# Wider dense products, paired weight-gradient products and VectorE copies in a two-layer attention decode backward pass

## The chip, the cores and the metric

The kernel runs on one core of a Trainium2 chip. The metric is the device time in microseconds (us) of one execution.

## The reference

Two attention blocks and two feed-forward blocks share their weights (A and B), one token goes through, and the outputs are the result and all gradients. Cut to what matters:

```python
Hq, Hkv, Sk, Dh, D, F = 32, 4, 65536, 128, 1024, 3584      # bf16
def A(x, k_cache, v_cache, wq, wo):                         # one query token
    q = (x @ wq) ...; p = softmax(q @ k.T * Dh**-0.5); return (p @ v) @ wo
def B(x, w1, b1, w2, b2):
    r = relu(x @ w1 + b1); return (r * r) @ w2 + b2
x = x + A(ln(x), ...); x = x + B(ln(x), ...)
x = x + A(ln(x), ...); x = x + B(ln(x), ...)
outputs = x, and vjp(grad_out) for x, k_cache, v_cache, wq, wo, w1, b1, w2, b2
```

The caches are 67 MB each. Both are read in each of four passes, and their gradients (again 134 MB) are written in the last.

## The kernel before

It makes four passes over the caches: forward of layer one, forward of layer three, one backward pass that gives layer three's query gradient, and a last pass that gives layer one's and writes the cache gradients. Between passes lie *dense stages* (one, two and three below) with layer norm, wq, wo, w1 and w2. A weight is loaded in slabs (1 MB or 896 KB pieces). In the views PE is TensorE, the matrix engine, ACT is ScalarE, DVE is VectorE, POOL is GpSimd, and SPq is the queue that issues the loads. Matrix results go to PSUM tiles (`ps_` in the views), and a copy out of one is an eviction. A weight is used in one of two ways. `g_mv` holds a 128x128 block of the weight still and streams the vector, one column wide ("block products"). `Rows` is for products with the transposed weight: it transposes eight blocks on PE, copies them to SBUF and multiplies ("row products"), or does the piece on VectorE, as a balancer decides.

```python
def g_mv(slab_it, nk, nbk, xcol, ps, finish, ...):
    for kc, slab in slab_it:
        for nb in range(nbk):
            nc.tensor.matmul(ps[:, nb:nb + 1], lhsT=cols(slab, nb), rhs=xcol(kc), start=first, stop=last, ...)
        add_load(pe=nbk * 0.064)
# Rows.front: transpose to PSUM, evac (copy) to wt; Rows.back:
for i in range(w):
    nc.tensor.matmul(job["y"][:, kc, q:q + 1], lhsT=wt[:, i, :], rhs=job["vb"][:, k0 + i:k0 + i + 1], ...)
# last pass: outer products of two rows, 512 columns, evicted by ScalarE or VectorE
def rank2(out, ra, rb):
    pg = ps_gg()                                  # four such PSUM tiles, shared with the cache gradients
    nc.tensor.matmul(pg[:, 0:n], lhsT=ra, rhs=rb, start=True, stop=True)
    evac(out, pg[:, 0:n], kind="f32")
# background work of the last pass runs up to six steps ahead of an even spread
while self.normal and self.done < self.total * i / self.steps + 6: ...
```

All 1 MB tiles (cache blocks, slabs, staged outputs) share 12 slots. A slot whose tile was stored is passed over for `STORE_STEPS = 5` steps, and seven cache blocks are kept from one pass to the next.

Of the kernel before, what the change touches and what calls it, by code (L numbers as in the profile page):

```python
# [16 lines left out]
P = 128  # L17
# [3 lines left out]
def kernel(  # L21
# [117 lines left out]
    def evac(out, in_, kind="bf"):  # L139
        n = 1  # L140
        for d in in_.shape[1:]:
            n *= d
        ca = 0.17 + n * 0.00083
        cd = 0.13 + n * (0.00054 if kind == "bf" else 0.00105)
        if load["act"] + ca <= load["dve"] + cd:
            load["act"] += ca
            nc.scalar.copy(out=out, in_=in_)  # L147
        else:
            load["dve"] += cd
            nc.vector.tensor_copy(out=out, in_=in_)  # L150
# [235 lines left out]
    def g_mv(slab_it, nk, nbk, xcol, ps, finish, side=None, pre=None, cols=None):  # L386
        first = True
        for kc, slab in slab_it:
            for nb in range(nbk):
                last = (kc == nk - 1) and (nb == nbk - 1)  # L390
                nc.tensor.matmul(ps[:, nb:nb + 1], lhsT=(cols or d_cols)(slab, nb), rhs=xcol(kc),
                                 start=first, stop=last, skip_group_check=True)
                first = False
            add_load(pe=nbk * 0.064)
            if side is not None:
                side(kc, slab)
            yield
        if pre is not None:
            pre()
        finish(ps)  # L400
        yield
# [57 lines left out]
    class Rows:  # L459
# [23 lines left out]
        def begin(self, job):  # L483
            npc = len(job["pieces"])
            job["vb"] = to_cols_bf(job["vcol"](), job["nj"])
            job["y"] = ps_acc([P, job["nk"], npc]) if PS["pass4"] else ps_bg([P, job["nk"], npc])
            if job["mix"]:
                nc.vector.memset(job["y"][:, :, :], 0.0)
                job["y2"] = tmp.tile([P, job["nk"], npc], F32, name="rows_y2", tag="rows_y2")
                nc.gpsimd.memset(job["y2"][:, :, :], 0.0)  # L490
                if job["vbc"] is None:
                    if npc > 1:
                        job["slot"] = Slot("s_vbc", True)
                        job["vbc"] = bcast_vec(job["vcol"](), job["nj"], job["slot"].t, f=job["cols"] is f_cols)
                    else:
                        job["vbc"] = bcast_vec(job["vcol"](), job["nj"])
                reset_load()

        def front(self, job, kc, slab):
            L = load  # L500
            for q, (k0, w) in enumerate(job["pieces"]):
                pe = w * 0.09
                if job["vbc"] is not None:
                    n = w * P
                    stt = max(L["dve"] + 0.1 + n * 0.00105, L["act"], L["pe"])
                    tra = max(L["dve"], L["act"] + 0.17 + n * 0.00083, L["pe"] + pe)
                    if stt <= tra:
                        if "y" not in job:
                            self.begin(job)
                        junk = mvs.tile([P, 1024], BF, name="mv_junk", tag="mv_t", bufs=2)  # L510
                        nc.vector.scalar_tensor_tensor(out=junk[:, 0:n], in0=slab[:, k0 * P:k0 * P + n], scalar=1.0,
                                                       in1=job["vbc"][:, k0 * P:k0 * P + n], op0=ALU.mult, op1=ALU.mult,
                                                       accum_out=job["y2"][:, kc, q:q + 1])
                        add_load(dve=0.1 + n * 0.00105)
                        self.did(job)
                        continue
                pt = self.ps_wt()
                for i in range(w):
                    nc.tensor.transpose(pt[:, i, :], job["cols"](slab, k0 + i), ident_b[:, :])  # L519
                if self.views:  # L520
                    wt = self.views.popleft()
                else:
                    wt = self.pool.tile([P, 8, P], BF, name="wt", tag="wt", bufs=self.bufs)
                evac(wt[:, 0:w, :], pt[:, 0:w, :])
                add_load(pe=pe)
                self.queue.append((job, kc, q, wt))
                if len(self.queue) >= self.bufs:
                    yield
# [8 lines left out]
        def back(self):  # L537
            job, kc, q, wt = self.queue.popleft()
            k0, w = job["pieces"][q]
            if "y" not in job:  # L540
                self.begin(job)
            for i in range(w):
                nc.tensor.matmul(job["y"][:, kc, q:q + 1], lhsT=wt[:, i, :], rhs=job["vb"][:, k0 + i:k0 + i + 1],
                                 start=(i == 0), stop=(i == w - 1), skip_group_check=True)
            self.did(job)

        def did(self, job):
            nk, npc = job["nk"], len(job["pieces"])
            job["done"] += 1
            if job["done"] == nk * npc:  # L550
                y = job["y"][:, :, :]
                if job["mix"]:
                    ym = tmp.tile([P, nk, npc], F32, name="rows_ym", tag="rows_ym")
                    nc.vector.tensor_tensor(out=ym[:, :, :], in0=y, in1=job["y2"][:, :, :], op=ALU.add)
                    y = ym[:, :, :]
                    if job["slot"] is not None:
                        job["slot"].free()
# [34 lines left out]
    class Background:  # L592
# [8 lines left out]
        def step(self, i):  # L601
# [10 lines left out]
            while self.normal and self.done < self.total * i / self.steps + 6:  # L612
# [76 lines left out]
    def g_q(L, g, ps=None, it=None):  # L689
        def fin(p):  # L690
            nc.vector.tensor_copy(out=L["qT"][:, gsl(g)], in_=p[:, :])
            nc.vector.tensor_copy(out=L["qpad"][:, g, :, :], in_=L["qT"][:, gsl(g)].unsqueeze(1).to_broadcast([P, 8, R]))
        yield from g_mv(it or wq_slabs(g)[0], DC, 8, lambda kc: L["nb"][:, kc:kc + 1],
                        ps_bg([P, 8]) if ps is None else ps, fin)


    def g_wo(L, xacc, g, ps=None, it=None):
        def fin(p):
            nc.vector.tensor_tensor(out=xacc[:], in0=xacc[:], in1=p[:, :], op=ALU.add)
        yield from g_mv(it or wo_slabs(g)[0], R, 8, lambda kc: L["oTb"][:, g * R + kc:g * R + kc + 1],  # L700
                        ps_bg([P, 8]) if ps is None else ps, fin)
# [398 lines left out]
    def rows2(cols, j0, jn, rows, f=False):  # L1100
        cc = tmp.tile([P, 4, 2], BF, name="r2_cc")
        for l in range(2):
            nc.vector.tensor_copy(out=cc[:, 0:jn, l], in_=cols[l][:, j0:j0 + jn])
        pg = ps_gg()
        for jj in range(jn):
            nc.tensor.matmul(pg[0:2, jj * P:(jj + 1) * P], lhsT=cc[:, jj, :], rhs=ident_b[:, :], start=True, stop=True)
        if f:
            evac(rows.rearrange("r (p j) -> r p j", j=4), pg[0:2, 0:jn * P].rearrange("r (j p) -> r p j", j=4), kind="f32")
        else:
            evac(rows, pg[0:2, 0:jn * P], kind="f32")  # L1110

    def rank2(out, ra, rb):
        pg = ps_gg()
        n = out.shape[-1]
        nc.tensor.matmul(pg[:, 0:n], lhsT=ra, rhs=rb, start=True, stop=True)  # L1115
        evac(out, pg[:, 0:n], kind="f32")

    def g_outer(pool, out_dram, nA, nB, a_cols, b_cols, c0=0, a_f=False):

        rb = pool.tile([2, 8 * P], BF, name="rowb", tag="rowb")  # L1120
        for k in range(0, nB, 4):
            rows2(b_cols, k, 4, rb[0:2, k * P:(k + 4) * P])
            yield
        for a0 in range(0, nA, 4):
            ra = pool.tile([2, 4 * P], BF, name="rowa", tag="rowa", bufs=2)
            rows2(a_cols, a0, 4, ra[0:2, :])
# [3 lines left out]
            for j in range(4):  # L1130
                for n0 in range(0, 1024, 512):
                    rank2(og[:, j, n0:n0 + 512], d_cols(ra, j) if a_f else f_cols(ra, j), rb[:, n0:n0 + 512])
# [6 lines left out]
    def g_outer_wide(pool, out_dram, nA, nB, a_cols, b_cols):  # L1139
# [3 lines left out]
        for k in range(0, nB, 4):  # L1143
            rows2(b_cols, k, 4, rb[0:2, k * P:(k + 4) * P], f=True)
            yield
        for a in range(nA):
            if a % 4 == 0:
                ra = pool.tile([2, 4 * P], BF, name="rowa", tag="rowa", bufs=2)
                rows2(a_cols, a, 4, ra[0:2, :])
                yield  # L1150
            sl = Slot("og", True)
            for n0 in range(0, nB * P, 512):
                rank2(sl.t[:, n0:n0 + 512], ra[:, (a % 4) * P:(a % 4 + 1) * P], rb[0:2, n0:n0 + 512])
                if n0 % 1024 == 512:
# [6 lines left out]
    def n_outer(nA, nB, wide=False):  # L1161
        return nB // 4 + nA // 4 + nA * (-(-nB // 8)) if wide else nB // 4 + nA // 4 * 5
# [18 lines left out]
    def ffn_act(ps, name):  # L1181
        h = tmp.tile([P, FC], F32, name="ffn_h")
        nc.vector.tensor_tensor(out=h[:], in0=ps[:, :], in1=b1c, op=ALU.add)
# [13 lines left out]
    def g_w2(L, xin, xout, ps, side=None):  # L1197
        def fin(p):
            f = tmp.tile([P, DC], F32, name="ffn_f")
            nc.vector.tensor_tensor(out=f[:], in0=p[:, :], in1=b2c[:], op=ALU.add)  # L1200
# [5 lines left out]
    run(g_q(L1, 0))  # L1206
# [23 lines left out]
    run(g_wo(L1, x1, lastg[0], ps_mv([P, 8]), PRE["wo1"]))  # L1230
    L2 = dict(name="L2")
    L2["n"], L2["nb"], L2["rstd"] = ln_fwd(x1, "L2")
    run(g_w1(L2, ps_mv([P, FC])))
# [13 lines left out]
    run(g_w2(L2, x1, x2, ps_mv([P, DC]), side=side))  # L1247
# [3 lines left out]
    run(g_q(L3, firstg[1], ps_mv([P, 8])))  # L1251
# [17 lines left out]
    run(g_wo(L3, x3, lastg[1], ps_mv([P, 8]), PRE["wo3"]))  # L1269
# [11 lines left out]
    run(g_w1(L4, ps_mv([P, FC]), pre=rows.fill))  # L1281
# [10 lines left out]
    def g_out0():  # L1292
        yield from g_w2(L4, x3, x4, ps_bg([P, DC]))
# [123 lines left out]
```

## Time and profile before

| | before |
|---|---|
| time | 2043.65 us (2043.44 to 2045.18, 3 runs) |
| span of the profiled run | 2033.9 us |
| moved by DMA | 803.5 MB, mean 395 GB/s |

The page cuts the span into 40 slices of 51 us. The digits are tenths: the granted TensorE clock, the mean busy share of the DMA engines; the last row is what they moved.

```profile
PEclk9999899679899997898999987999788997789988
DMA  9999999999999998999999985999999999999995
GB/s 384 419 411 416 415 415 418 377 350 414 414 414 416 415 405 324 397 417 413 416 414 415 418 313 214 370 423 424 423 381 424 423 423 409 425 416 423 423 376 213
```

DMA is full except in slices (counted from 0) 7-8, 15, 23-24 and at the end: the three dense stages and the tail. In the dense stages the clock is low too. The windows view shows it for the stretches in which weights are multiplied (columns: stretch, its length, busy us of PE, weight load, VectorE, ScalarE and GpSimd with instruction counts, granted clock, DMA share, GB/s):

```profile
384.00:428.00 44.00, 29.48 (x660) 28.25 (x658) 24.59 (x56) 10.39 (x12) 0.15 (x1) 0.50 0.93 365
812.00:824.00 12.00, 9.24 (x120) 8.52 (x118) 5.75 (x16) 6.14 (x7) 0.12 (x1) 0.51 1.00 374
1200.00:1250.00 50.00, 44.13 (x779) 41.23 (x777) 34.50 (x79) 29.11 (x34) 0.00 (x0) 0.76 0.71 270
```

The chain of waits in dense stage one (start, us, what; L391 are block products, L519 transposes, L543 row products):

```profile
377.22 1.76 PE ps_mv L391 x64
382.68 3.88 PE ps_mv L391 x112
386.57 9.68 DMA s_w<-in_B_w_dram
...
407.57 0.64 PE ps_mv L391 x24
408.21 0.89 PE ps_tr L519 x8
409.12 1.02 ACT wt L147
410.19 0.37 PE ps_bg L543 x8
...
424.38 1.85 PE ps_mv L391 x64
```

Eight transposes take 0.89 us at half clock. At full clock, in stage three, the same group takes 0.47 us (for one, at 1195.52). The two groups of 64 are wo and the next q, 28 to 29 ns a product (1.76 and 1.85 us by 64). The rows from 407 to 410 are a chain in which PE and one copy alternate.

### The profile page before, as it was taken

How to read it: one execution, taken by the hardware profiler on the slowest of the kernel's cores; microseconds unless marked ns; L12 is line 12 of the kernel's file. 1: busy time of each engine (PE TensorE's matmuls, PEld its weight loads, DVE VectorE, ACT ScalarE, POOL GpSimd, SP SyncE). 2: the span in 40 equal slices, each digit the busy share in tenths (PEclk: the TensorE clock that was granted, in tenths of full speed). 3: DMA queues.
4: the chain of work that ended last, by engine and by line, in shares of the span. 5: the costliest groups of instructions: out<-in, count | busy, mean ns of one | idle time of the engine just before them, and what ended most of it. 6: DMA issues, size and time to landing. Idle time of an engine off the chain costs nothing.

```text
span 2033.9 us, 68654 instructions
## 1 busy us (share of the span) xinstructions
PE 1695.0 (83%) x30590; PEld 1340.7 (66%) x30590; DVE 1207.2 (59%) x2535; ACT 1125.0 (55%) x2035; POOL 90.9 (4%) x189
## 2 busy tenths in 40 slices
PE   6788877688888886887977879989799989998887
PEld 6777777677877776876876777545455545555554
DVE  4444454355444443455464346879687977788776
ACT  3544454245444543345354345778577876677765
POOL 0000000000000000000000000101011110111111
PEclk9999899679899997898999987999788997789988
DMA  9999999999999998999999985999999999999995
GB/s 384 419 411 416 415 415 418 377 350 414 414 414 416 415 405 324 397 417 413 416 414 415 418 313 214 370 423 424 423 381 424 423 423 409 425 416 423 423 376 213
DMA packets 136535, 803.48 MB, mean 395 GB/s; under 512 B 12448, under 2 KB 12462, under 8 KB 52398
## 3 DMA queue, kind: packets, MB, share of 16 engines
q1 hardware_dynamic: 112190, 633.39, 76.8%
q0 software_dynamic: 24048, 165.70, 19.6%
q8 instruction: 239, 3.92, 0.8%
q14 instruction: 58, 0.48, 0.1%
HBM read 633.35 MB, written 165.69 MB: 393 GB/s over the span
## 4 chain that ended last, share of the span: by engine, by line
PE 46%; DMA 26%; ACT 15%; DVE 9%; issue 4%; SPq 0%; ACTq 0%; POOLq 0%; DVEq 0%
DMA blk_v<-in_A_v_cache_dram 15%; PE ps_tr L758 7%; ACT E L815 6%; PE ps_sc L776 5%; PE ps_tr L1010 5%; PE ps_gg L1058 5%; ACT kt L147 4%; PE ps_acc L842 4%; DMA blk_k<-in_A_k_cache_dram 4%; DMA out_dram<-gstk 3%; DVE kt L150 3%; PE ps_gg L1115 3%; PE ps_tr L901 3%; PE ps_sc L1039 2%; PE ps_tr L519 2%
## 5 line engine op out<-in xcount | busy, mean ns | idle before, releaser
L150 DVE COPY kt<-ps_tr 128x1024 bf16<-128x1024 bf16 x676 | 456.2, 688 | 330.6 <-PE ps_tr L758 148.8
L147 ACT COPY kt<-ps_tr 128x1024 bf16<-128x1024 bf16 x348 | 352.4, 1025 | 419.4 <-PE ps_tr L758 217.5
L758 PE MATMUL ps_tr<-ident_b,blk_k 128*128 128x128 bf16 x4096 | 300.1, 227 | 5.5 <-DMA blk_k<-in_A_k_cache_dram 3.2
L758 PEld LDWEIGHTS <-blk_k 128*128 128x128 bf16 x4096 | 251.8, 102 | 7.5 <-DMA blk_k<-in_A_k_cache_dram 3.8
L776 PE MATMUL ps_sc<-L_qpad,kt 128*128 128x64 bf16 (+7 forms) x4096 | 199.2, 195 | 64.9 <-DVE kt L150 40.9
L1058 PE MATMUL ps_gg<-GG,xt 64*128 64x512 bf16 x1024 | 212.6, 415 | 17.0 <-DVE og L150 8.5
L147 ACT CAST gstk<-ps_gg 128x512 bf16<-128x512 f32 x340 | 181.7, 595 | 80.3 <-PE ps_gg L1058 74.0
L776 PEld LDWEIGHTS <-kt 128*128 128x128 bf16 x4096 | 160.3, 100 | 82.8 <-DVE kt L150 49.0
L1010 PE MATMUL ps_tr<-ident_b,blk_v 128*128 128x128 bf16 x2048 | 189.7, 235 | 19.2 <-DMA blk_v<-in_A_v_cache_dram 17.8
L1010 PEld LDWEIGHTS <-blk_v 128*128 128x128 bf16 x2048 | 133.0, 105 | 109.6 <-issue 83.0
L842 PE MATMUL ps_acc<-E,blk_v 128*128 128x64 bf16 (+4 forms) x4096 | 174.0, 199 | 20.8 <-ACT L_fw L863 8.3
L147 ACT CAST gstv<-ps_gg 128x512 bf16<-128x512 f32 x289 | 156.2, 600 | 39.8 <-PE ps_gg L1058 39.4
L815 ACT ACTIVATE E<-S_sb,L_negm 128x128 bf16<-128x128 f32 x256 | 150.3, 989 | 39.6 <-DVE L_negm L811 39.6
L842 PEld LDWEIGHTS <-blk_v 128*128 128x128 bf16 x4096 | 150.4, 103 | 23.3 <-issue 20.7
L150 DVE CAST gstv<-ps_gg 128x512 bf16<-128x512 f32 x223 | 145.4, 685 | 34.1 <-PE ps_gg L1058 31.7
L901 PE MATMUL ps_tr<-ident_b,blk_v 128*128 128x128 bf16 x2048 | 145.1, 225 | 13.1 <-DMA blk_v<-in_A_v_cache_dram 11.2
L1085 PEld LDWEIGHTS <-blk_k 128*128 128x128 bf16 x2048 | 83.4, 101 | 93.7 <-issue 80.2
L901 PEld LDWEIGHTS <-blk_v 128*128 128x128 bf16 x2048 | 122.4, 101 | 29.8 <-DMA blk_v<-in_A_v_cache_dram 19.1
L1085 PE MATMUL ps_acc<-X,blk_k 128*128 128x64 bf16 (+3 forms) x2048 | 115.8, 197 | 10.9 <-DMA blk_k<-in_A_k_cache_dram 10.9
L150 DVE CAST gstk<-ps_gg 128x512 bf16<-128x512 f32 x172 | 113.4, 684 | 19.0 <-PE ps_gg L1058 15.7
L921 PE MATMUL ps_sc<-dOpad,kt 128*128 128x64 bf16 (+7 forms) x2048 | 101.4, 194 | 27.7 <-ACT kt L147 15.2
L815 ACT ACTIVATION_READ_ACCUMULATOR E<-S_sb,L_negm 128x1 f32 x256 | 123.3, 482 | 0.0
(267 smaller groups left out, 2199.0 us busy)
## 6 DMA issues: line engine op xcount, KB each, us to landing
blk_k<-in_A_k_cache_dram SPq DMA_DIRECT2D x248, 1024.0 KB, 20.0
blk_v<-in_A_v_cache_dram SPq DMA_DIRECT2D x243, 1024.0 KB, 20.0
out_dram<-gstv POOLq DMA_DIRECT2D x64, 1024.0 KB, 13.6
out_dram<-gstk POOLq DMA_DIRECT2D x64, 1024.0 KB, 13.3
s_wq<-in_A_wq_dram SPq DMA_DIRECT2D x32, 1024.0 KB, 20.0
s_wo<-in_A_wo_dram SPq DMA_DIRECT2D x32, 1024.0 KB, 20.2
s_w<-in_B_w_dram SPq DMA_DIRECT2D x32, 896.0 KB, 7.6
out_dram<-og POOLq DMA_DIRECT2D x23, 1024.0 KB, 14.3
```

Source lines behind the costliest of these rows:

```text
L147: nc.scalar.copy(out=out, in_=in_)
L150: nc.vector.tensor_copy(out=out, in_=in_)
L758: nc.tensor.transpose(pt[:, i, :], kb8[:, i, :], ident_b[:, :])
L776: nc.tensor.matmul(state["ps_s"][:, s:s + w, :].rearrange("p a b -> p (a b)"), lhsT=kt[:, i, :], rhs=L["qpad"][:, g, 0:w, :].rearrange("p ...
L815: nc.scalar.activation(out=E(g, c0, SU)[:, :, L["lr"].start + h], in_=S[:, h, :], func=ACTF.Exp, bias=negm[:, g, su, h:h + 1], scale=SCALE ...
L842: nc.tensor.matmul(ps_o[:, 0:w, :], lhsT=vb8[:, i, :], rhs=E(g, c, w)[:, :, lr], start=(c % SU == 0), stop=(c % SU == SU - 1), skip_group_ ...
L901: nc.tensor.transpose(pt[:, i, :], vb8[:, i, :], ident_b[:, :])
L921: nc.tensor.matmul(state["ps_dp"][:, s:s + w, :].rearrange("p a b -> p (a b)"), lhsT=vt[:, i, :], rhs=dOpad[:, g, 0:w, :].rearrange("p a b ...
L1010: nc.tensor.transpose(pt[:, i, :], vb8[:, i, :], ident_b[:, :])
L1058: nc.tensor.matmul(pgs[h][:, :], lhsT=xt[64 * h:64 * h + 64, j1 // 8 + m, :], rhs=gg[64 * h:64 * h + 64, :, :].rearrange("p a b -> p (a b) ...
L1085: nc.tensor.matmul(ps_dq[:, 0:w, :].rearrange("p a b -> p (a b)"), lhsT=kb8[:, i, :], rhs=X[:, s:s + w, :].rearrange("p a b -> p (a b)"), ...
L1115: nc.tensor.matmul(pg[:, 0:n], lhsT=ra, rhs=rb, start=True, stop=True)
```

## The change

The intent: keep the PE clock up in the dense stages by making the products wider, take PE and ScalarE time out of the last pass, and spread the background work evenly. Cut to its core:

```diff
 def evac(...):
+    if PS["pass4"] and kind == "bf":
+        ca += 1.5                              # bf16 copies of the last pass go to VectorE
 def g_mv(...):
+    rep = 1 if ps_of is ps_bg else min(64, 512 // nbk)     # 64; 18 for w1
+    ps = ps_of([P, rep, nbk])
-            nc.tensor.matmul(ps[:, nb:nb + 1], lhsT=..., rhs=xcol(kc), ...)
-        add_load(pe=nbk * 0.064)
+            nc.tensor.matmul(ps[:, :, nb], lhsT=..., rhs=xcol(kc).to_broadcast([P, rep]), ...)
+        add_load(pe=nbk * 0.03)
-    finish(ps)
+    finish(ps[:, 0, :])
 # Rows.back: column c and the 63 after it (overwritten by later products, masked where VectorE did the piece)
-    nc.tensor.matmul(job["y"][:, kc, q:q + 1], lhsT=wt[:, i, :], rhs=vb, ...)
+    nc.tensor.matmul(job["ps"][:, c:c + 64], lhsT=wt[:, i, :], rhs=vb.to_broadcast([P, 64]), ...)
 # Background.step
-    while self.normal and self.done < self.total * i / self.steps + 6:
+    while self.normal and self.done < self.total * i / self.steps:
 # weight gradients: rows at partitions 0 and 64, two products on two row groups
+    for h, o in enumerate(outs):
+        r = slice(64 * h, 64 * h + 2)
+        nc.tensor.matmul(pgs[h][:, :], lhsT=lhs(r), rhs=rhs(r), ..., tile_position=(64 * h, 0))
```
(cuts: the row tiles that are made twice, the mask, and bookkeeping)

More of the change, by code (lines that the diff above doesn't have):

```diff
@@ L144, in evac @@
         cd = 0.13 + n * (0.00054 if kind == "bf" else 0.00105)
+        if PS["pass4"] and kind == "bf":
+            ca += 1.5
         if load["act"] + ca <= load["dve"] + cd:
-            load["act"] += ca
+            load["act"] += 0.17 + n * 0.00083
             nc.scalar.copy(out=out, in_=in_)
@@ L384, in w2_slabs, with g_mv @@
         return slabs("s_w2", lambda k, kn: v[:, k // 4, :, :], FC, 4, D, ahead)
-    def g_mv(slab_it, nk, nbk, xcol, ps, finish, side=None, pre=None, cols=None):
+    def g_mv(slab_it, nk, nbk, xcol, ps_of, finish, side=None, pre=None, cols=d_cols):
+        rep = 1 if ps_of is ps_bg else min(64, 512 // nbk)
+        ps = ps_of([P, rep, nbk])
         first = True
@@ L390, in g_mv @@
                 last = (kc == nk - 1) and (nb == nbk - 1)
-                nc.tensor.matmul(ps[:, nb:nb + 1], lhsT=(cols or d_cols)(slab, nb), rhs=xcol(kc),
+                nc.tensor.matmul(ps[:, :, nb], lhsT=cols(slab, nb), rhs=xcol(kc).to_broadcast([P, rep]),
                                  start=first, stop=last, skip_group_check=True)
                 first = False
-            add_load(pe=nbk * 0.064)
+            add_load(pe=nbk * 0.03)
             if side is not None:
@@ L485, in begin @@
             job["vb"] = to_cols_bf(job["vcol"](), job["nj"])
-            job["y"] = ps_acc([P, job["nk"], npc]) if PS["pass4"] else ps_bg([P, job["nk"], npc])
+            ny = job["nk"] * npc
+            job["rep"] = 64 if not job["mix"] or ny <= 32 else 1
+            job["ps"] = (ps_acc if PS["pass4"] else ps_bg)([P, ny + 64])
+            job["y"] = job["ps"][:, 0:ny].rearrange("p (k q) -> p k q", q=npc)
             if job["mix"]:
-                nc.vector.memset(job["y"][:, :, :], 0.0)
+                job["mask"] = tmp.tile([P, job["nk"], npc], F32, name="rows_m", tag="rows_m", bufs=1)
+                nc.gpsimd.memset(job["mask"][:, :, :], 1.0)
+                nc.vector.memset(job["ps"][:, 0:ny], 0.0)
                 job["y2"] = tmp.tile([P, job["nk"], npc], F32, name="rows_y2", tag="rows_y2")
@@ L501, in front @@
             for q, (k0, w) in enumerate(job["pieces"]):
-                pe = w * 0.09
+                pe = w * 0.1
                 if job["vbc"] is not None:
@@ L513, in front @@
                                                        accum_out=job["y2"][:, kc, q:q + 1])
+                        nc.gpsimd.memset(job["mask"][:, kc, q:q + 1], 0.0)
                         add_load(dve=0.1 + n * 0.00105)
@@ L542, in back @@
             for i in range(w):
-                nc.tensor.matmul(job["y"][:, kc, q:q + 1], lhsT=wt[:, i, :], rhs=job["vb"][:, k0 + i:k0 + i + 1],
+                c = kc * len(job["pieces"]) + q
+                nc.tensor.matmul(job["ps"][:, c:c + job["rep"]], lhsT=wt[:, i, :],
+                                 rhs=job["vb"][:, k0 + i:k0 + i + 1].to_broadcast([P, job["rep"]]),
                                  start=(i == 0), stop=(i == w - 1), skip_group_check=True)
@@ L553, in did @@
                     ym = tmp.tile([P, nk, npc], F32, name="rows_ym", tag="rows_ym")
-                    nc.vector.tensor_tensor(out=ym[:, :, :], in0=y, in1=job["y2"][:, :, :], op=ALU.add)
+                    nc.vector.tensor_tensor(out=ym[:, :, :], in0=y, in1=job["mask"][:, :, :], op=ALU.mult)
+                    nc.vector.tensor_tensor(out=ym[:, :, :], in0=ym[:, :, :], in1=job["y2"][:, :, :], op=ALU.add)
                     y = ym[:, :, :]
@@ L686, in gsl, with g_q, g_wo @@
         return slice(g * R, (g + 1) * R)
-    def g_q(L, g, ps=None, it=None):
+    def g_q(L, g, ps=ps_bg, it=None):
         def fin(p):
-            nc.vector.tensor_copy(out=L["qT"][:, gsl(g)], in_=p[:, :])
+            nc.vector.tensor_copy(out=L["qT"][:, gsl(g)], in_=p)
             nc.vector.tensor_copy(out=L["qpad"][:, g, :, :], in_=L["qT"][:, gsl(g)].unsqueeze(1).to_broadcast([P, 8, R]))
         yield from g_mv(it or wq_slabs(g)[0], DC, 8, lambda kc: L["nb"][:, kc:kc + 1],
-                        ps_bg([P, 8]) if ps is None else ps, fin)
-    def g_wo(L, xacc, g, ps=None, it=None):
+                        ps, fin)
+    def g_wo(L, xacc, g, ps=ps_bg, it=None):
         def fin(p):
-            nc.vector.tensor_tensor(out=xacc[:], in0=xacc[:], in1=p[:, :], op=ALU.add)
+            nc.vector.tensor_tensor(out=xacc[:], in0=xacc[:], in1=p, op=ALU.add)
         yield from g_mv(it or wo_slabs(g)[0], R, 8, lambda kc: L["oTb"][:, g * R + kc:g * R + kc + 1],
-                        ps_bg([P, 8]) if ps is None else ps, fin)
+                        ps, fin)
     def dO_finish(L, g):
@@ L1097, in attn_bwd4, with rows2 @@
         pipeline(items, [(vT, 0), (vS, TLEAD), (dV8, DV_LAG), (k8, B4_LAG)], bg, end)
-    def rows2(cols, j0, jn, rows, f=False):
-        cc = tmp.tile([P, 4, 2], BF, name="r2_cc")
-        for l in range(2):
-            nc.vector.tensor_copy(out=cc[:, 0:jn, l], in_=cols[l][:, j0:j0 + jn])
+    def rows2(cols, halves, rows, f=False):
+        cc = tmp.tile([P, 2, 4, 2], BF, name="r2_cc")
         pg = ps_gg()
-        for jj in range(jn):
-            nc.tensor.matmul(pg[0:2, jj * P:(jj + 1) * P], lhsT=cc[:, jj, :], rhs=ident_b[:, :], start=True, stop=True)
-        if f:
-            evac(rows.rearrange("r (p j) -> r p j", j=4), pg[0:2, 0:jn * P].rearrange("r (j p) -> r p j", j=4), kind="f32")
-        else:
-            evac(rows, pg[0:2, 0:jn * P], kind="f32")
@@ L1112, in rank2 @@
-    def rank2(out, ra, rb):
-        pg = ps_gg()
-        n = out.shape[-1]
-        nc.tensor.matmul(pg[:, 0:n], lhsT=ra, rhs=rb, start=True, stop=True)
-        evac(out, pg[:, 0:n], kind="f32")
+        for h, j0 in enumerate(halves):
+            for l in range(2):
+                nc.vector.tensor_copy(out=cc[:, h, :, l], in_=cols[l][:, j0:j0 + 4])
+            for jj in range(4):
+                nc.tensor.matmul(pg[64 * h:64 * h + 2, jj * P:(jj + 1) * P], lhsT=cc[:, h, jj, :], rhs=ident_b[:, :],
+                                 start=True, stop=True, tile_position=(0, 64 * h))
@@ new lines, in rows2, with rank2 @@
+        for h in range(len(halves)):
+            r = slice(64 * h, 64 * h + 2)
+            if f:
+                evac(rows[r, :].rearrange("r (p j) -> r p j", j=4), pg[r, :].rearrange("r (j p) -> r p j", j=4), kind="f32")
+            else:
+                evac(rows[r, :], pg[r, :], kind="f32")
+    def rank2(outs, lhs, rhs):
+        pgs = [ps_gg() for _ in outs]
+        for h, o in enumerate(outs):
+            r = slice(64 * h, 64 * h + 2)
+            nc.tensor.matmul(pgs[h][:, :], lhsT=lhs(r), rhs=rhs(r), start=True, stop=True, tile_position=(64 * h, 0))
+        for pg, o in zip(pgs, outs):
+            evac(o, pg[:, :], kind="f32")
@@ L1118, in g_outer @@
     def g_outer(pool, out_dram, nA, nB, a_cols, b_cols, c0=0, a_f=False):
-        rb = pool.tile([2, 8 * P], BF, name="rowb", tag="rowb")
-        for k in range(0, nB, 4):
-            rows2(b_cols, k, 4, rb[0:2, k * P:(k + 4) * P])
-            yield
+        rb = pool.tile([66, 4 * P], BF, name="rowb", tag="rowb")
+        rows2(b_cols, (0, 4), rb)
+        yield
         for a0 in range(0, nA, 4):
-            ra = pool.tile([2, 4 * P], BF, name="rowa", tag="rowa", bufs=2)
-            rows2(a_cols, a0, 4, ra[0:2, :])
+            ra = pool.tile([66, 4 * P], BF, name="rowa", tag="rowa", bufs=2)
+            rows2(a_cols, (a0, a0), ra)
@@ L1130, in g_outer @@
             for j in range(4):
-                for n0 in range(0, 1024, 512):
-                    rank2(og[:, j, n0:n0 + 512], d_cols(ra, j) if a_f else f_cols(ra, j), rb[:, n0:n0 + 512])
+                rank2([og[:, j, 0:512], og[:, j, 512:1024]], lambda r: d_cols(ra[r, :], j) if a_f else f_cols(ra[r, :], j), lambda r: rb[r, :])
                 if j < 3:
@@ L1142, in g_outer_wide @@
         rb = rsl.t
-        for k in range(0, nB, 4):
-            rows2(b_cols, k, 4, rb[0:2, k * P:(k + 4) * P], f=True)
+        for k in range(0, nB, 8):
+            rows2(b_cols, (k, k + 4) if k + 4 < nB else (k,), rb[0:66, k * 64:k * 64 + 512], f=True)
             yield
@@ L1147, in g_outer_wide @@
             if a % 4 == 0:
-                ra = pool.tile([2, 4 * P], BF, name="rowa", tag="rowa", bufs=2)
-                rows2(a_cols, a, 4, ra[0:2, :])
+                ra = pool.tile([66, 4 * P], BF, name="rowa", tag="rowa", bufs=2)
+                rows2(a_cols, (a, a), ra)
                 yield
             sl = Slot("og", True)
-            for n0 in range(0, nB * P, 512):
-                rank2(sl.t[:, n0:n0 + 512], ra[:, (a % 4) * P:(a % 4 + 1) * P], rb[0:2, n0:n0 + 512])
-                if n0 % 1024 == 512:
+            for k in range(0, nB, 8):
+                outs = [sl.t[:, (k + 4 * h) * P:(k + 4 * h + 4) * P] for h in range(2) if k + 4 * h < nB]
+                rank2(outs, lambda r: d_cols(ra[r, :], a % 4), lambda r: rb[r, k * 64:k * 64 + 512])
+                if k + 8 < nB:
                     yield
@@ L1161, in n_outer @@
     def n_outer(nA, nB, wide=False):
-        return nB // 4 + nA // 4 + nA * (-(-nB // 8)) if wide else nB // 4 + nA // 4 * 5
+        return -(-nB // 8) + nA // 4 + nA * (-(-nB // 8)) if wide else 1 + nA // 4 * 5
     psA_stack = ExitStack()
@@ L1182, in ffn_act @@
         h = tmp.tile([P, FC], F32, name="ffn_h")
-        nc.vector.tensor_tensor(out=h[:], in0=ps[:, :], in1=b1c, op=ALU.add)
+        nc.vector.tensor_tensor(out=h[:], in0=ps, in1=b1c, op=ALU.add)
         r = vec.tile([P, FC], F32, name=name + "_r")
@@ L1199, in fin @@
             f = tmp.tile([P, DC], F32, name="ffn_f")
-            nc.vector.tensor_tensor(out=f[:], in0=p[:, :], in1=b2c[:], op=ALU.add)
+            nc.vector.tensor_tensor(out=f[:], in0=p, in1=b2c[:], op=ALU.add)
             nc.vector.tensor_tensor(out=xout[:], in0=xin[:], in1=f[:], op=ALU.add)
@@ L1205 @@
     L1["n"], L1["nb"], L1["rstd"] = ln_fwd(x0, "L1")
-    run(g_q(L1, 0))
+    run(g_q(L1, 0, ps_mv))
     nc.vector.tensor_copy(out=x1[:], in_=x0[:])
@@ L1229 @@
     gxbc = bcast_vec(gx[:], DC)
-    run(g_wo(L1, x1, lastg[0], ps_mv([P, 8]), PRE["wo1"]))
+    run(g_wo(L1, x1, lastg[0], ps_mv, PRE["wo1"]))
     L2 = dict(name="L2")
     L2["n"], L2["nb"], L2["rstd"] = ln_fwd(x1, "L2")
-    run(g_w1(L2, ps_mv([P, FC])))
+    run(g_w1(L2, ps_mv))
     x2 = vec.tile([P, DC], F32, name="x2")
@@ L1246, in side @@
             rows.back()
-    run(g_w2(L2, x1, x2, ps_mv([P, DC]), side=side))
+    run(g_w2(L2, x1, x2, ps_mv, side=side))
     while rows.queue:
@@ L1250 @@
     L3["n"], L3["nb"], L3["rstd"] = ln_fwd(x2, "L3")
-    run(g_q(L3, firstg[1], ps_mv([P, 8])))
+    run(g_q(L3, firstg[1], ps_mv))
     nc.vector.tensor_copy(out=x3[:], in_=x2[:])
@@ L1268 @@
     dst = open_dense("dense23")
-    run(g_wo(L3, x3, lastg[1], ps_mv([P, 8]), PRE["wo3"]))
+    run(g_wo(L3, x3, lastg[1], ps_mv, PRE["wo3"]))
     L4 = dict(name="L4")
@@ L1280 @@
     rows.add(wo_slabs(firstg[2])[0], R, DC, lambda: dx3[:], dO_finish(L3, firstg[2]))
-    run(g_w1(L4, ps_mv([P, FC]), pre=rows.fill))
+    run(g_w1(L4, ps_mv, pre=rows.fill))
     nc.vector.scalar_tensor_tensor(out=dh4[:], in0=dg4[:], scalar=2.0, in1=L4["r"][:], op0=ALU.mult, op1=ALU.mult)
@@ L1292, in g_out0 @@
     def g_out0():
-        yield from g_w2(L4, x3, x4, ps_bg([P, DC]))
+        yield from g_w2(L4, x3, x4, ps_bg)
         col_to_dram(x4, D, out_0.rearrange("a b d -> (a b d)"))
```

## The prediction

> **What bounds the kernel now.** The page shows 803.5 MB over 2033.9 us. The stretch-by-stretch table shows a DMA share of 0.99 to 1.02 in nearly all of the four cache passes; there a faster engine is worth nothing. Summing (1.0 minus DMA share) gives about 88 us of idle DMA: 8 us at 360-430 (dense stage one), 10 at 768-828 (two), 36 at 1190-1280 (three, and the first blocks of the last pass), 29 after 1958 (tail), 4 at the start. Only these can be won; over 2% (41 us) needs half of them.
>
> In the gaps PE leads the chain of waits. Granted clock is 0.50 in 384-428 and 812-824, mean about 0.76 in 1200-1250. There eight 128-column transposes take 0.88 us in the chain, 0.47 us at clock 1.00. [...]
>
> **The change, costed.**
> 1. Repeated vectors: some 1,400 dense products become 64 (w1: 18) columns wide. The passes' 64-column products stand 33 ns apart warm, 54 cold: +9 or +19 ns each. In return the clock should stay near 1.0. Chain of 1190-1250: about 150 cold transposes lose 7 us, about 340 products gain 3: net -4 us. Stage two: -2. Stage one (cold w2 phase): -3. The short wo and q bursts (64 products, 1.8 us) get no faster. Mask memsets are on GpSimd; the mask multiply adds 0.2 us three times.
> 2. Last pass, bf16 copies to VectorE: the built order shows 75 `kt` and 82 `xt` copies leaving ScalarE (1025 to 688 ns, 600 to 415 ns) and 146 casts going to it (685 to 595 ns): 50 us of engine time saved, against some 25 more row evictions of 0.6 us. The pass is DMA-bound and the tail's chain is PE: -1 us.
> 3. Pairs on two row groups: 240 products of 512 columns, 0.32 us each in the chain, overlap two by two. PE saves about 35 us and pays 100 more 128-column products (6 us). Off the critical path except at pass start and tail: -2 us.
> 4. Background steps no longer run six ahead: row and outer products on the chain at 1255-1265 (3.5 us) leave it, and staging takes slots later, so loads resume sooner: -4 us. About six more steps fall into the PE-bound tail: +2 us.
>
> The tail also holds an accident: an eviction into a reused slot waits for a store from 1934 to 1958; all engines idle from 1951 to 1958. Moved steps may remove, keep or lengthen that, +-7 us.
>
> Sum: about -15 us. Predicted 2028 us; 8 in 10 within 2009 to 2043. Faster by over 2%: 0.10; within: 0.88; slower: 0.02.
>
> **What would show it.** (1) Clock 0.85 or more in the dense stages; transposes near 0.47 us per eight; stage three 3 to 6 us shorter. (2) Last pass: few bf16 copies on ScalarE, both engines less busy, DMA share still 1.0 and its middle equally long. (3) Pairs start together; PE busy falls with no gain in time. (4) First store of the last pass 2 to 4 us sooner after its start, the DMA hole of 1250-1263 smaller. (5) Passes one to three unchanged within 1%.
>
> **What would make it wrong.** The clock stays low in the dense stages[...]: then wider products cost 3 to 8 us. Or the warm clock shortens the copy chain more than I count, worth 10 us more. Or another slot wait in the tail.

-4, -2 and -3 for the dense stages, 0.6 for the mask multiply, -1, -2, -4 and +2 come to -13.4 us, put as about -15 and as 2028 us, 15.6 us under before. That wider products would raise the clock was my estimate. The trace of before goes with it, and shows no more: the clock is 0.86 to 1.00 in each 50 us from 50 to 350 and from 450 to 750, where the products with the caches are 64 and 128 columns wide, and 0.50 in dense stage one, with block products of one column. The +9 and +19 ns also use the spacing of one-column products: 24 ns at full clock (32 in 0.78 us from 1194.74) and 35 at half (112 in 3.88 us from 382.68), against 33 (32 in 1.07 us from 375.50, clock 0.92) and 54 (eight in 0.43 us from 428.81, clock 0.52 over 428 to 430).

## The result

| | before | changed |
|---|---|---|
| time, four runs each | 2043.55 us (2038.15 to 2045.18) | 2037.16 us (2036.18 to 2038.32) |
| ratio | 1 | 0.9974 (95%: 0.9954 to 0.9993) |

A ratio is the mean time of one kernel's fast runs over that of the other's of the same rounds, so not quite the ratio of the medians. The gain is real but a third of the forecast: 0.26% of 2043.6 is 5 us, where 15.6 us had been predicted.

The page after:

```profile
PEclk9999899799899996999999988988988998698898
DMA  9999999999999998999999986999999999999995
GB/s 384 416 410 414 413 414 415 360 335 406 411 414 413 413 415 323 398 415 410 416 412 414 416 338 231 375 424 393 422 424 424 423 423 404 423 415 423 423 371 212
```

The windows view of the three dense stretches:

```profile
400.00:427.00 27.00, 25.48 (x449) 24.71 (x447) 17.73 (x38) 13.16 (x13) 0.00 (x0) 0.92 0.95 362
810.00:830.00 20.00, 16.06 (x305) 14.33 (x303) 15.95 (x37) 13.71 (x17) 0.48 (x9) 1.00 0.84 311
1205.00:1255.00 50.00, 45.17 (x831) 42.20 (x827) 36.41 (x90) 30.77 (x36) 0.48 (x10) 0.86 0.85 309
```

The clock rose as intended, from 0.50, 0.51 and 0.76 to 0.92, 1.00 and 0.86. The stretches are not the same ones: over the stretches of before the changed kernel has 0.84 (384 to 428), 1.00 and 0.84. Yet slices 7-8 moved less than before (360 and 335 GB/s against 377 and 350): stage one got slower. Its chain, with L397 for block products, L532 for transposes and L557 for row products:

```profile
378.77 3.75 PE ps_mv L397 x64
385.81 3.91 PE ps_mv L397 x112
389.73 9.70 DMA s_w<-in_B_w_dram
...
408.58 0.45 PE ps_mv L397 x8
409.02 0.45 PE ps_tr L532 x8
409.47 0.89 PE ps_mv L397 x16
410.36 0.46 PE ps_tr L532 x8
410.85 1.02 ACT wt L150
411.91 0.23 PE ps_bg L557 x2
...
428.24 5.21 PE ps_mv L397 x64
```

The transposes fell to 0.45 us as forecast. But eight block products now take 0.45 us, as long as eight transposes of 128 columns, and the bursts of wo and q grew from 1.76 and 1.85 us to 3.75 and 5.21 us. Row products, also 64 wide, are cheap. From the chain of stage three:

```profile
1211.56 0.25 PE ps_bg L557 x8
1211.81 0.45 PE ps_tr L532 x8
```

Lengths of stages in the traces (us, from the first instruction of each to that of the next; stage one is from the wo burst to the first transpose of the next pass, stage two and pass three stand together because DMA binds their sum: its share over 850 to 1150 is 1.02 before and changed):

| profile | stage one | pass two | two + pass three | stage three | last pass | span |
|---|---|---|---|---|---|---|
| before | 48.9 | 350.8 | 412.8 | 61.1 | 783.1 | 2033.9 |
| before, again | 49.0 | 348.5 | 418.2 | 60.7 | 781.5 | 2035.7 |
| changed | 54.5 | 348.6 | 415.7 | 58.2 | 780.2 | 2035.9 |
| changed, again | 53.4 | 347.9 | 416.7 | 55.6 | 781.4 | 2034.0 |

The first profile of before is a quick one: its own time was 2035.69 us, 8 us below its median. So the stages, not the spans, are compared: stage one +5, stage three -3 to -5, the last pass -0.1 to -2.9. The four profiles do not show the 5 us as a whole: their spans are level, and the gain in time rests on the rounds.

### The profile page after: what moved, and what is told of

Same layout as the page of the kernel before. It is cut to its first block, busy times and chain, and to the rows that moved or that the text cites. A ratio compares the mean times of both kernels' runs of the same rounds, so it can differ in the third digit from the quotient of the medians.

```text
span 2035.9 us, 69009 instructions
## 1 busy us (share of the span) xinstructions
PE 1689.3 (83%) x30754; PEld 1344.3 (66%) x30754; DVE 1188.6 (58%) x2586; ACT 1103.0 (54%) x2063; POOL 92.4 (5%) x232
## 4 chain that ended last, share of the span: by engine, by line
PE 45%; DMA 28%; ACT 15%; DVE 8%; issue 4%; SPq 0%; ACTq 0%; POOLq 0%; DVEq 0%; POOL 0%
DMA blk_v<-in_A_v_cache_dram 13%; PE ps_tr L774 7%; ACT E L831 6%; DMA blk_k<-in_A_k_cache_dram 5%; PE ps_sc L792 5%; PE ps_tr L1026 4%; PE ps_gg L1074 4%; PE ps_acc L858 4%; ACT kt L150 4%; PE ps_tr L917 3%; DVE kt L153 3%; DMA out_dram<-og 3%; PE ps_gg L1139 2%; DMA out_dram<-gstk 2%; PE ps_mv L397 2%
## 5 line engine op out<-in xcount | busy, mean ns | idle before, releaser
L153 DVE COPY kt<-ps_tr 128x1024 bf16<-128x1024 bf16 x751 | 507.3, 687 | 340.6 <-PE ps_tr L774 145.4
L150 ACT COPY kt<-ps_tr 128x1024 bf16<-128x1024 bf16 x273 | 275.7, 1024 | 410.9 <-PE ps_tr L774 230.0
L150 ACT CAST gstk<-ps_gg 128x512 bf16<-128x512 f32 x396 | 207.6, 600 | 99.7 <-PE ps_gg L1074 78.5
L150 ACT CAST gstv<-ps_gg 128x512 bf16<-128x512 f32 x379 | 199.2, 601 | 100.1 <-PE ps_gg L1074 99.2
L1026 PE MATMUL ps_tr<-ident_b,blk_v 128*128 128x128 bf16 x2048 | 183.0, 230 | 20.1 <-DMA blk_v<-in_A_v_cache_dram 18.9
L858 PEld LDWEIGHTS <-blk_v 128*128 128x128 bf16 x4096 | 152.9, 103 | 36.4 <-issue 31.3
L917 PE MATMUL ps_tr<-ident_b,blk_v 128*128 128x128 bf16 x2048 | 143.7, 224 | 14.3 <-DMA blk_v<-in_A_v_cache_dram 12.0
L937 PE MATMUL ps_sc<-dOpad,kt 128*128 128x64 bf16 (+7 forms) x2048 | 100.7, 194 | 26.6 <-ACT kt L150 15.5
L1055 PE MATMUL ps_sc<-DOB,kt 128*128 128x64 bf16 (+3 forms) x2048 | 111.3, 198 | 0.2 <-DVE kt L153 0.2
L153 DVE CAST gstv<-ps_gg 128x512 bf16<-128x512 f32 x133 | 90.0, 684 | 28.1 <-PE ps_gg L1074 27.7
```

The costliest lines, as they stand in the source:

```text
L150: nc.scalar.copy(out=out, in_=in_)
L153: nc.vector.tensor_copy(out=out, in_=in_)
L858: nc.tensor.matmul(ps_o[:, 0:w, :], lhsT=vb8[:, i, :], rhs=E(g, c, w)[:, :, lr], start=(c % SU == 0), stop=(c % SU == SU - 1), skip_group_ ...
L917: nc.tensor.transpose(pt[:, i, :], vb8[:, i, :], ident_b[:, :])
L937: nc.tensor.matmul(state["ps_dp"][:, s:s + w, :].rearrange("p a b -> p (a b)"), lhsT=vt[:, i, :], rhs=dOpad[:, g, 0:w, :].rearrange("p a b ...
L1026: nc.tensor.transpose(pt[:, i, :], vb8[:, i, :], ident_b[:, :])
```

## The experiments

All gave correct results and ran in 5 rounds with runs of before on the same chip, unless said otherwise. They ran in four groups on four chips (to mv_strides; to nolead_only; to contig_lead_st10; the last three), so ratios of different groups are compared only through before.

**before_again** (the kernel before, unedited, 3 rounds).

> The kernel before itself, as a null run. Ratio to before 1.000 within 0.2%. It also says how far one program's single runs lie apart (2035.7 to 2045.2 us so far) and where in the trace two runs of it differ; if the tail or a slot wait moves by several us between two profiles of the same program, differences of that size between the profiles of before and after are not the change's.

Measured: 1.0002 (0.9976 to 1.0028), single runs 2034.6 to 2041.6 us. Two profiles agree within 2.4 us in each stage except stage two with pass three (5 us apart). A difference of a few us in one profile of that part, or of the whole, is not the change's. Three later kernels leave the dense stages as before (pairs_only, dve_only, nolead_only); over these five profiles stage one takes 48.9 to 50.8 us and stage three 60.7 to 63.3.

**mv_contig**

```diff
-ps = ps_of([P, rep, nbk])   ...  ps[:, :, nb]   ...  finish(ps[:, 0, :])
+ps = ps_of([P, nbk, rep])   ...  ps[:, nb, :]   ...  finish(ps[:, :, 0])
```

> The changed kernel, but the 64 repeated results of a block lie next to each other in PSUM, not 8 elements apart. Theory (the stride of the output doubles the time of a repeated product): 64-wide block products fall from 56 to about 33 ns apart at full clock, the wo burst from 3.8-4.3 to 2.1-3.5 us, the q burst from 5.2 to 2.1-3.5 us, dense stage one from 56.7 to about 51 us; total 5 to 8 us under the changed kernel, about 2030 us. Rival (the repeated operand or accumulation over 64 columns costs it): still 56 ns, time as changed.

Measured: 2028.13 us, ratio 0.9951 (0.9931 to 0.9971). Stage one 47.1 us. Its chain:

```profile
378.89 2.16 PE ps_mv L397 x64
...
412.95 0.24 PE ps_mv L397 x8
413.19 0.46 PE ps_sc L532 x8
...
423.41 2.76 PE ps_mv L397 x64
```

Eight products fell from 0.45 to 0.24 us with nothing changed but where their results lie. The theory holds, the rival falls. The operand is repeated as before, so repetition is not the cost. The ratio is 0.0023 to 0.0030 under the two of the changed kernel, on other chips and with intervals that overlap; the reading rests on the spacing and on stage one.

**mv_single**

```diff
-rep = 1 if ps_of is ps_bg else min(64, 512 // nbk)
+rep = 1
```

> The changed kernel with block products one column wide again; all else stays. Theory (the strided repeats cost more than the clock they buy): 24 ns (warm) to 35 ns (cold) apart, bursts 1.8 us again, but the clock falls to 0.5 in part of dense stage one; total 2 to 6 us under the changed kernel. Rival (repeats are needed for the clock): dense stage one no shorter than 56 us and total at or above the changed kernel.

Measured: 2033.48 us, 0.9979 (0.9960 to 0.9997), level with the changed kernel; stage one 53.1 us. Neither side was right. The bursts are 1.79 and 1.85 us again, but the w2 phase ran cold: eight transposes took 0.88 us, with products 0.19. Strided repeats gave back, in w2 and the bursts, about what they won. (The balancer still counts 0.030 us for a block product here; single_pe, below, puts that back.)

**mv_strides** (one look)

```diff
+st = LAYOUTS.popleft()                        # 4, 1, 2, 4, 2 for q, wo, w2, q, wo
+pt4 = ps_of([P, nbk // st, 64, st]); outs = [pt4[:, b // st, :, b % st] for b in range(nbk)]
```

> One look at several output strides in one program: first q 4 elements, first wo 1, w2 2, second q 4, second wo 2. If the stride sets the cost, eight products of w2 at full clock take (stride 2) between 0.27 and 0.45 us, the bursts order by stride at equal clock; if any stride above 1 costs the same[...], stride 2 gives 0.45 us per eight.

Measured: wo contiguous 2.16 us and w2 two apart in the chain:

```profile
378.91 2.16 PE ps_mv L406 x64
...
402.60 0.85 PE ps_mv L406 x8
404.02 0.45 PE ps_mv L406 x8
...
414.74 0.45 PE ps_mv L406 x8
415.19 0.45 PE ps_sc L543 x8
```

Two apart costs 0.45 us per eight at full clock and 0.85 cold, the same as eight apart; contiguous is 0.25 and 0.43. The q burst four apart took 5.36 us (84 ns a product, between the 56 at full clock and 106 cold of the others), against 2.76 contiguous in mv_contig. So it is not a cost that grows with distance: at 2, 4 and 8 elements apart a column costs about double, a factor of 1.8 to 2.0.

**rows_only** (the kernel before, with the `Rows` part of the change alone).

> The kernel before with the row products alone repeated over 64 columns (outputs next to each other). Theory: the clock rises in dense stage three and eight transposes in the chain fall from 0.88 to 0.45 us; that stage goes from 60.9 to 55-58 us, stage two stays at 51-56 (its chain then waits for slabs from DMA), stage one 47-50 (its block products stay one column wide); total 2 to 6 us under before. Rival (the stage is bound by DMA and by the copies on ScalarE, the clock is a bystander): stage three within 1 us of 60.9.

Measured: 2028.34 us, 0.9941 (0.9922 to 0.9960): more than the whole change. Stage three 53.5 us in place of 60.7 to 63.3; its windows view:

```profile
1203.00:1249.00 46.00, 40.21 (x831) 37.39 (x828) 36.53 (x94) 30.70 (x36) 0.48 (x10) 1.00 0.84 315
```

The clock is full there, and idle DMA in the 60 us ahead of the last pass fell from 17.9 to 10.0 us. Stage two with pass three took 412.5 us, no gain: in stage two the warm chain runs into slabs that have not landed (6.60 us from 804.75, 9.87 us from 817.70), as in the changed kernel, whose chain reads

```profile
812.15 4.58 DMA s_w<-in_B_w_dram
...
819.56 9.94 DMA s_wo<-in_A_wo_dram
```

The last pass was 776.7 us, 5 us shorter, in this profile; little in it was edited, and why it was shorter is open. In stage one, where the block products stay one column wide, wider row products did not raise the clock: 0.50 over 384 to 428 as before, and the stage took 51.5 us, over its forecast of 47 to 50.

**pairs_only** (the kernel before, with the paired outer products alone).

> The kernel before with the weight gradient pairs alone. Theory: about 18 us less PE busy time over the last pass, which DMA bounds, so the last pass stays within 1 us of the 781.5-783.1 us of before, total within 0.1%. Rival (the pairs are the gain of the last pass): last pass 2 to 3 us shorter.

Measured: 2041.05 us, 0.9994 (0.9976 to 1.0013); last pass 785.1 us. PE busy time over 1300-1950 is 572.2 us, against 582.3 and 571.8 in the two profiles of before, so even the PE saving drowns in their spread. In the changed kernel's trace most pairs do not run together: counted over the trace, 17 of 116 pairs start within 0.2 us of each other (40 in pairs_only), and in 48 other products stand between the two (timeline: start, us, count, idle before and what ended it):

```profile
1283.15 0.39 PE L1139 MATMUL ps_gg<-rowb,rowa 2*128 2x512 bf16 x2
1288.14 0.37 PE L1139 MATMUL ps_gg<-rowb,rowa 2*128 2x512 bf16 x1 [0.29 <-ACT gstk L150]
1288.45 0.34 PE L1026 MATMUL ps_tr<-ident_b,blk_v 128*128 128x128 bf16 x3
1288.72 0.38 PE L1139 MATMUL ps_gg<-rowb,rowa 2*128 2x512 bf16 x1
```

The pair at 1283 runs side by side in 0.39 us; that at 1288 starts 0.58 us apart, with three transposes in between. Its first product waited for an eviction; that waits for one of the four PSUM tiles are what parts the pairs is a guess, not shown.

**dve_only** (the kernel before, with the copy rule alone).

> The kernel before with bf16 copies of the last pass on VectorE alone. Theory: ScalarE some 20 us and VectorE some 5 to 15 us less busy over the last pass, last pass 0 to 1.5 us shorter (only its start and tail are not DMA-bound). Rival: the copies are the gain of the last pass, 2 to 3 us.

Measured: 2039.35 us, 0.9991 (0.9969 to 1.0013). Over 1300-1950 ScalarE is busy 451.0 us in place of 476.5, VectorE 496.9 in place of 514.1: 43 us of engine time saved, and no gain that the interval shows; DMA share there is 1.01 in both.

**nolead_only**

```diff
-while self.normal and self.done < self.total * i / self.steps + 6:
+while self.normal and self.done < self.total * i / self.steps:
```

> The kernel before with background steps no longer six ahead, alone. Theory: first store of the last pass 9 to 11 us after its first transpose in place of 12.2; the steps come back in the tail, last transpose to end 37-40 us in place of 36.9; last pass 0 to 3 us shorter. Rival (they all come back in the tail): last pass 781-784 us, first store earlier all the same.

Measured: 2046.30 us, 1.0025 (1.0005 to 1.0045): slower, by an interval that only just leaves 1 out. The last pass is 784.5 us in the profile (before 783.1 and 781.5). The first store does come sooner, 10.0 us into the pass in place of 12.2. But idle DMA in the first 30 us is 17.8 us (before 17.3 and 16.3), while after 700 us it is 31.3 (27.9, 27.4), and between 30 and 620 us 5.9 (2.9, 2.6). The rival was right, if anything stronger than stated: the sooner store won nothing at the start, and idle DMA grew later. At the start, loads wait for the first store to *land*. That is what the queue's own waits say (total, times, longest, in us), of this kernel from 1256 on:

```profile
SPq L279 <- DMA out_dram<-gstv: 26.6, 1, 26.6
```

of the changed kernel from 1255 on:

```profile
SPq L282 <- DMA out_dram<-gstv: 28.6, 1, 28.6
```

and of before from 1250 on:

```profile
SPq L279 <- DMA out_dram<-gstv: 36.5, 2, 26.3
```

**after_again** (the changed kernel, unedited, beside the next three).

> The changed kernel again, to stand on one chip beside the next three. Ratio to before 0.997 within 0.2%. From the single parts (rows 0.9941, pairs 0.9994, copies 0.9991, no lead 1.0025) and block products that are no gain with strided outputs, the product is 0.995.

Measured: 2035.43 us, 0.9981 (0.9963 to 0.9998). The product of the single parts, 0.9941 x 0.9994 x 0.9991 x 1.0025 = 0.9951, is what the change would give if the parts multiply and the strided block products were neither gain nor loss; the difference, 0.3%, is then theirs. Each factor has an interval of about 0.2% to either side, so this is an estimate.

**contig_lead** (mv_contig with `+ 6` again).

> The changed kernel with both faults mended: results next to each other, background steps six ahead again. If the parts add up: rows -0.6%, block products -0.2 to -0.3%, pairs and copies -0.1%: ratio 0.990 to 0.992, 4 to 6 us under the contiguous kernel with no lead (0.9951). If the lead costs nothing once the dense stages are shorter, 0.995.

Measured: 2023.15 us, 0.9915 (0.9897 to 0.9933). The two mends together count. That each does is likely, not clear of noise: mv_contig, with the first alone, has 0.9951 (0.9931 to 0.9971) on another chip. This kernel beats the one before and the changed one, by 17 and 13 us in ratio on the same chip. Against mv_contig, idle DMA after 700 us of the last pass is 26.0 us in place of 29.2, the same 3 us as between before and nolead_only. The profile is of the slowest of the six runs (2032.50 us), so its stages may not stand for the others.

**dense_contig** (contig_lead with the copy rule and the outer products of before).

> The kernel before with only the dense stages changed (rows repeated, block products repeated with results next to each other); last pass as before. Theory: this carries nearly the whole gain: ratio 0.991 to 0.993. Rival (pairs and copies matter in company): 0.994 or more.

Measured: 2025.65 us, 0.9935 (0.9916 to 0.9954). This lies between the two forecasts. The dense stages alone carry about three quarters of the gain; the intervals of this and contig_lead overlap, so it is not shown that pairs and copies add anything. Nor is it shown that the wider block products add anything in time, even with their results next to each other: rows_only, which leaves them one column wide, has 0.9941 on its chip. They do shorten stage one: 45.6 to 48.2 us in five profiles with contiguous repeats, against 51.5 in rows_only and 48.9 to 50.8 where it is unedited.

**contig_lead_st10** (contig_lead with `STORE_STEPS = 10`).

> As the mended kernel, but a slot whose tile was just stored is passed over for ten steps in place of five, so that staging tiles and loads take slots whose store has landed. Theory (the waits of the tail on stores of reused slots cost time): idle DMA after 700 us of the last pass falls from 28 to below 24 us, total 3 to 8 us under the mended kernel. Rival (slots run short and loads start later): middle of the pass idle, same or slower.

Measured: 2035.88 us, 0.9985 (0.9967 to 1.0002). Half the theory came true: idle DMA after 700 us fell from 26.0 to 18.4 us. But between 30 and 620 us it rose from 4.8 to 16.4, and the last pass took 793.3 us in place of 783.0, so the rival decided.

**contig_w2**

```diff
-rep = 1 if ps_of is ps_bg else min(64, 512 // nbk)
+rep = 64 if ps_of is not ps_bg and nk == FC else 1
```

> The mended kernel (results next to each other, lead of six) with block products repeated only in the long stream of w2; the bursts of 64 (q, wo) and w1 are one column wide. Theory: the bursts start cold, where 64 columns cost 54 ns against 29: wo and q bursts back to 1.8-1.9 us, start and stage two 1.5 to 2 us shorter each, w2 phase as quick as in the mended kernel; ratio 0.989 to 0.991 (mended 0.9915). Rival (the short bursts warm the clock for what follows): stage one 2 us or more longer, ratio 0.992 or more.

Measured: 2026.57 us, 0.9943 (0.9921 to 0.9965). Stage one took 45.6 us (contig_lead 48.2) and stage two with pass three 413.8 (415.1). The signs are the theory's, but five profiles with the mended stage one spread over 45.6 to 48.2 us, so this shows nothing. The time shows no gain, against a forecast of 0.989 to 0.991; the mended kernel was not run on this chip. Inconclusive; nor is it shown that short bursts warm the clock.

**single_pe** (mv_single with `add_load(pe=nbk * 0.064)`).

> Block products one column wide, with the balancer's old cost of 0.064 us for each in place of 0.030; else as the kernel with one-wide block products (0.9979, stage one 53.1 us). Theory (the lower cost alone sent more pieces to the cold PE and ScalarE): stage one 49 to 51.5 us, total 1 to 4 us lower. Rival (it was noise between runs): stage one 53, same ratio.

Measured: 2029.90 us, 0.9968 (0.9942 to 0.9995) against 0.9979; stage one 50.5 us in place of 53.1. The stage agrees with the theory (a block product that the balancer takes for cheaper draws work to a PE that is slow), but profiles of one code spread over as much as 2.6 us here, so one profile of each does not show it. The total is within noise.

**contig_lead24** (contig_lead with `+ 24`).

> The mended kernel with background steps up to 24 ahead in place of 6. If no lead cost 5 us because steps fall into the tail, more lead takes steps out of the tail: idle DMA after 700 us of the last pass below 26 us and the total 1 to 5 us under the mended kernel. Rival (at lead six the tail holds none of them any more, and a bigger lead only crowds the start of the pass): same or slower, idle in the first 30 us above 17 us.

Measured: 2024.77 us, 0.9935 (0.9913 to 0.9956), and idle DMA after 700 us 29.0 us. No gain over six is seen, with intervals that overlap and contig_lead on another chip. So the cost of no lead is shown in time by nolead_only, and mv_contig and contig_lead agree. That it falls in the tail is not shown: after 700 us, mv_strides without lead has 25.6 us of idle DMA, and this kernel, with a lead of 24, 29.0. What turns on the lead stays open.

## Why the prediction was wrong

Its picture of the whole held: DMA bounds the passes (share 1.02 over 850 to 1150, 1.01 over 1300 to 1950, before and changed), only some 88 us of idle DMA can be won, the gain is well under 2%, and the measured 2037.16 us lies inside the range. Its gain of 15.6 us was three times the measured 5 us. That the miss was no larger is partly luck: the row products alone gave 12 us (rows_only), of which 5, in a last pass hardly edited, have no explanation, and made up for part of what follows. The steps:

1. *"The passes' 64-column products stand 33 ns apart warm, 54 cold: +9 or +19 ns each."* This is the term that failed. It holds for the row products (0.25 us per eight, 31 ns each), not for the block products, which came out 56 ns apart warm and 106 cold (0.45 and 0.85 us per eight), because their results lie eight elements apart in PSUM (next to each other, in mv_contig, 0.24 and 0.43). The passes' products, from which I took the number, write next to each other. Forecast for stage one -3 us, measured +5.5 and +4.4. mv_contig, which changes the layout alone, took it to 47.1 us.
2. *"The short wo and q bursts ... get no faster."* They became 2 to 3.4 us slower each in stage one. Even contiguous, the stage-one q burst took 2.76 us against 1.85.
3. *The clock stays near 1.0.* Right in the main: 0.92, 1.00, 0.86 (0.84 over all of 384 to 428). Stage three was forecast at -4 us and gave -3 to -5 in the changed kernel, -7 in rows_only. *Stage two: -2* was wrong: a warm chain there waits for slabs (4.58 and 9.94 us in the changed kernel), and gained 0 in rows_only; what the chain waits for next has to be read from the trace. What sets the clock is not shown. In stage one it went with the time that PE is shown busy: over 400 to 427 18.75 of 27 us at 0.50 before, 25.48 at 0.92 changed. But in stage three PE was shown busy for 44.13 of 50 us at 0.76 before, and for 40.21 of 46 at 1.00 in rows_only: the share shown as busy does not tell the clock. With the width of the products it went like this: with the row products alone 64 columns wide, stage three rose from 0.76 to 1.00 (rows_only, 1203 to 1249), while stage one stayed at 0.50 over 384 to 428 (in mv_single, with the same widths, eight transposes there took 0.88 us); with the block products 64 wide as well, stage one ran at 0.92 over 400 to 427 (changed) and 1.00 over 404 to 424 (mv_contig). No run measured at what width the clock rises, or what the transposes do to it.
4. *Background steps, -4 + 2.* Wrong in sign: nolead_only is 0.25% (5 us; interval 0.05 to 0.45%) slower. The first store came 2 us sooner as forecast, but loads wait for it to land (26.6 us in nolead_only), and idle DMA in the first 30 us did not shrink. The estimate took steps off the chain at the pass start without asking what the loads waited for.
5. *Copies -1, pairs -2.* Copies: 43 us of engine time saved (50 forecast), no gain shown in time. Pairs: no gain shown; 17 of 116 pairs start within 0.2 us of each other.
6. *The tail accident.* Stores before a reused slot stayed: the changed kernel's chain has waits of 19.65 us from 1936.90 and 11.35 us from 1991.99 on such stores, before had 23.99 from 1933.98. It did not decide the result: the last pass is within 3 us.

As a sum of single parts: rows -0.59%, pairs -0.06%, copies -0.09%, no lead +0.25% make -0.5%; measured -0.26 and -0.19%. The +0.2 to +0.3% between them is put down to the strided block products. That is a remainder, but mv_contig, where only their layout is changed, comes to -0.49%.

## What to carry to other kernels

Widening a product to keep the PE clock up can cost more than the clock gives back: here a column cost about double where results were not written next to each other (eight products 0.45 us against 0.24 at full clock). Lay repeats out innermost, and check one group's spacing in the trace before counting on a number taken from another layout. Where DMA bounds a pass, look first at what the loads wait for: a first store that comes sooner, or 43 us less copying, changed nothing that the runs show. When several edits go in together, time each alone; here one of them was worth more than all, and two (the strided block products, the lost lead) cancelled it in part.
